# The intermediate words of a float64 conversion move from SBUF to PSUM, and the zero tile gets a place of its own

## The chip, the core and the metric

The kernel runs on one core of a Trainium2 chip. A core has five engines that run side by side and meet through semaphores: TensorE (PE, matmuls into PSUM), VectorE (DVE), ScalarE (ACT), GpSimd (POOL) and SyncE (SP, which here only issues DMAs). SBUF is the large working memory, PSUM the small one of eight banks into which PE writes. The metric is the time of one execution on the device in microseconds (us), the median of several.

## The reference

Three stages follow each other, all in float32 on 2304 tokens (4 batches of 576) of width 512:

```
attention:  8 heads of 64; scores = q k^T / 8 + decay (a difference of prefix sums of log f), causal, softmax, @ v
first MoE:  h = max(x @ w1, x @ w2, x @ w3)  (512 x 768 each);   x = h @ w_out  (768 x 512)
second MoE: gate logits + noise, the best 2 of 8 experts per token;  out += weight * (relu(x @ e1[e]) @ e2[e])
```

The weights of the first MoE (w1, w2, w3, w_out) arrive as float64. They are read as pairs of 32-bit words, and float32 values are made of them on the chip with integer operations.

## The kernel before

The tokens are cut into eight units, two per batch: 256 tokens (scores against 256 keys) and 320 tokens (against 576). Each unit passes through attention, in steps of one tile of up to 128 rows, then the first MoE, then gating; the experts follow when all units are through. All queues are written out by hand: a Python generator issues attention in half steps, and between them the loop over units issues the first MoE's matmuls in 22 groups (18 for the three products, 4 for w_out), so that the attention of the next unit stands between the groups of this one. To keep float32 accuracy most products are made of three matmuls (`three`, L659) on values split into a high and a low part.

The weights of the first MoE are converted in 24 pieces while attention of the first units runs. A piece is a tile `wr` or `raw` of 128 rows with 512 float64 values (two tiles of 256 in two of the late pieces). `w_load` loads it, and `piece` (L325) turns it into float32 with three integer instructions on DVE, with pauses between them:

- L334 shifts the upper words left by 3 and masks them, from the raw tile into the tile `sw`;
- L336 takes sign and top bit of the upper words, ors `sw` into them, and writes them over the upper words in the raw tile;
- L338 shifts the lower words right by 29 and ors the upper words into them, again over the upper words.

Then `split` (L303) writes the high part on ACT (L304) and the low part on POOL (L305). Both words are read with a step of two, since they lie side by side. `sw` is one SBUF buffer of the pool `stg`; the 26 uses (20 tiles `wr` and 2 `raw` of 512 columns, 4 `raw` of 256) share it one after the other. `w_step` issues 0.75 steps of conversion per half step of attention before the first MoE and 1.15 beside it, so the conversions spread over unit 0's and unit 1's attention and end beside unit 0's first MoE.

That MoE sums into tiles `m` (`mtile`, L656) of the PSUM pool `ps_m`, which has three banks used in turn. L680 (ACT) and L682 (DVE) take the maximum of three such sums. Of the attention steps, L457 is DVE's row minimum of the scores, L461 ACT's exponential, L466 and L467 DVE's reciprocal, L469 POOL's scaling, L476 PE's transposes, L488 ACT's copy of them, L530 the product with V in plain float32 for the first 16 heads, and L236 (POOL) and L237 (DVE) the split of q and k for the next head.

`zero_dram` (L149) takes the same buffer as `sw` for a tile `zt` of zeros once the conversions are through, clears `meta` and the first rows of `x2d`, and clears the output in 19 stores of 256 KB, one per three groups of the first MoE from unit 1 on.

Of the kernel before, what the change touches and what calls it, by code (L numbers as in the profile page):

```python
# [8 lines left out]
F32 = mybir.dt.float32  # L9
# [12 lines left out]
DM = 512  # L22
# [11 lines left out]
LN_EXP_SET = [x.name for x in SETS].index("natural_log_exp_and_others")  # L34
XBUF = 8            # attention outputs kept (hi and lo) for the first MoE
STB = 3             # staging buffers
RATE0, RATE1 = 0.75, 1.15   # steps of weight conversion per half step of attention, before and in the first MoE
W0 = 4              # attention step from which weights are converted
WE, PF0, PFD = 1, 4, 3      # weight pieces loaded at once, before conversions start, ahead of them
CN = 1              # attention step at which the decay prefixes are stored  # L40
ND = 4              # heads that get their prefix straight from SBUF
AH = 5              # heads by which the first split heads are loaded ahead
NV = 16             # heads whose P @ V runs in plain float32
LG = 20             # attention step at which the gate's inputs are loaded
VSH = 1             # steps by which V is split later
LEAD = (6, 2)       # attention steps of the next unit done beside a unit's first MoE
GG = 22             # groups of matmuls in a unit's first MoE
PPD, PPL, RSP = 5, 1, 1     # pauses in a unit's gating: before positions (last unit: PPL), between row tiles
HK, TE = (1, 3), (2, 5)     # places of interleaved work in expert 0's products
COLS = ((0, 2 * QA_N), (QA_N, QA_N + S + QB_N))  # L50
# [4 lines left out]
def moe_stack(ctx, tc, qk, v, f, w1, w2, w3, wo, wg, noise, e1, e2, out):  # L55
# [28 lines left out]
    with tc.manual_schedule():  # L84
# [3 lines left out]

        # -------------------------------------------------- attention buffers
        QKA = [ap_.tile([128, QB_N + S], F32R, name=f"QKA{i}") for i in range(2)]  # L90
# [8 lines left out]

        # ------------------------------------------------------ decay prefix  # L100
        BH = B * H
# [10 lines left out]

        # ---------------------------------------------------------- constants
        nc.gpsimd.memset(ident, 1.0)
# [34 lines left out]
        def zero_dram():  # L149
            zt = stg.tile([128, DM], F32, tag="sw", name="zt", bufs=1)  # L150
            nc.gpsimd.memset(zt, 0.0)
            nc.sync.dma_start(meta.rearrange("(p r) t -> p (r t)", p=128), zt[:, 0:NE * REG // 64])
            nc.sync.dma_start(x2d[0:PAD, :], zt)
            for r in range(NTOK // 128 + 1):
                yield
                nc.sync.dma_start(out[r * 128:(r + 1) * 128, :], zt)

        # ---------------------------------------------------------- attention
        XH, XL = {}, {}
# [136 lines left out]
        nc.gpsimd.tensor_scalar(CR[0][:, 1, 0:QA_N], L0.bitcast(F32), -1.0, 0.0, op0=OP.mult, op1=OP.add)  # L296
        # ------------------------------------------------------ MoE1 weights
        moe1_w = {}
# [26 lines left out]
        def piece(raws_, dt, hi_, lo_):  # L325
            n = hi_.free_size() // len(raws_)
            vals = []
            for raw in raws_:
                val = raw[:, 0:n]
                if dt == I64:  # L330
                    r2 = raw.bitcast(I32)[:, 0:2 * n].rearrange("p (c t) -> p c t", t=2)
                    low, top = r2[:, :, 0], r2[:, :, 1]
                    sw = stg.tile([128, 512], I32, tag="sw", name="sw", bufs=1)[:, 0:n]
                    nc.vector.tensor_scalar(sw, top, 3, 0x3FFFFFFF, op0=OP.logical_shift_left, op1=OP.bitwise_and)  # L334
                    yield
                    nc.vector.scalar_tensor_tensor(top, top, -0x40000000, sw, op0=OP.bitwise_and, op1=OP.bitwise_or)  # L336
                    yield
                    nc.vector.scalar_tensor_tensor(top, low, 29, top, op0=OP.logical_shift_right, op1=OP.bitwise_or)  # L338
                    val = raw[:, 0:2 * n].rearrange("p (c t) -> p c t", t=2)[:, :, 1]
                vals.append(val)  # L340
            yield
            for i, val in enumerate(vals):
                split(hi_[:, i * n:(i + 1) * n], lo_[:, i * n:(i + 1) * n], val, nc.gpsimd)
# [310 lines left out]

        # --------------------------------------------------------------- MoE1
        def mtile():  # L656
# [58 lines left out]

        # ------------------------------------------------------------- gating
        scatters = []
# [140 lines left out]

        # ------------------------------------------------------------ experts
        ex = {}  # L860
# [276 lines left out]

        # ------- tokens past the static slots of an expert, or in expert 0's first slots too late for them
        any_ = nc.values_load(anyi[0:1, 0:1], min_val=0, max_val=nxt_t + 1)
# [102 lines left out]
```

## Time and profile before

| | |
|---|---|
| median of 3 runs | 1074.23 us (1074.07 to 1074.79) |
| span of the profiled execution, first to last instruction | 1074.9 us |
| PE busy | 1032.7 us, 96% |
| DVE busy | 550.0 us, 51% |
| ACT busy | 522.2 us, 49% |
| POOL busy | 504.4 us, 47% |
[...]
| first x2T copy of unit 0's first MoE (L711) | 141.1 us |

The page gives no time of the profiled execution besides its span. Busy times are means over the whole span and hide stages; the views by stretch below don't. A matmul's end is modelled, so a busy PE may still contain short stalls. An instruction's duration holds the time in which it stands blocked in the engine, which is why the spread of equal instructions is worth a look.

### The profile page before, as it was taken

Reading aid. Unit: us, or ns where it says so; the run is one execution under the profiler, and the core shown is the slowest. Engines: PE = TensorE matmul, PEld = TensorE weight load, DVE = VectorE, ACT = ScalarE, POOL = GpSimd, SP = SyncE. Lnnn points to the kernel's source line nnn. Section 1 sums busy time; section 2 is a strip of 40 time slices with the busy share of each in tenths; the row PEclk is TensorE's granted clock in tenths of the full one; section 3 lists DMA queues with packets and bytes.
Section 4 is the critical chain, followed back from the end, with each engine's and each line's share of the span. In section 5 each row is a group of like instructions: output and inputs, shape, how many; then the busy total and the mean of one; then the engine's idle time right before and its main releaser. Section 6 shows DMA issues by size and latency. Waiting matters only on the chain.

```text
span 1074.9 us, 18911 instructions
## 1 busy us (share of the span) xinstructions
PE 1032.7 (96%) x6612; PEld 916.6 (85%) x6612; DVE 550.0 (51%) x1505; ACT 522.2 (49%) x1310; POOL 504.4 (47%) x573
## 2 busy tenths in 40 slices
PE   6899899999999999999999999999999999999996
PEld 3466688989989899898899988989898989899995
DVE  6999958658586585865635424323132323223210
ACT  5666656666566675666523334333333333333211
POOL 6778645544645446454327255343434252444202
PEclk9989999999999999999999999999999999999998
DMA  7764434232342212321013247363535354444203
GB/s 192 192 164 133 129 86 136 82 91 86 98 126 61 52 57 59 107 58 46 12 68 121 83 83 213 128 127 108 137 86 141 98 137 118 125 111 119 40 10 41
DMA packets 77167, 109.17 MB, mean 102 GB/s; under 512 B 37172, under 2 KB 38580, under 8 KB 77004
## 3 DMA queue, kind: packets, MB, share of 16 engines
q1 hardware_dynamic: 66828, 86.90, 27.6%
q0 software_dynamic: 10240, 21.02, 10.3%
q8 instruction: 54, 0.88, 0.3%
q14 instruction: 45, 0.37, 0.1%
HBM read 86.48 MB, written 21.39 MB: 100 GB/s over the span
## 4 chain that ended last, share of the span: by engine, by line
PE 74%; DVE 13%; DMA 4%; issue 3%; POOL 3%; ACT 1%; SPq 1%; POOLq 0%; DVEq 0%; ACTq 0%
PE m L660 8%; PE m L662 7%; PE m L661 7%; PE g L660 6%; PE g L661 6%; PE g L662 6%; PE m L973 6%; PE m L972 6%; PE m L971 6%; PE o L534 4%; PE pt L476 3%; DVE wr L336 2%; DVE QKB L237 2%; DMA wr<-in_w 2%; PE m L729 2%
## 5 line engine op out<-in xcount | busy, mean ns | idle before, releaser
L469 POOL TENSOR_SCALAR P<-P,stat 128x512 f32<-128x512 f32 (+4 forms) x160 | 101.4, 634 | 219.3 <-DVE stat L467 125.1
L660 PE MATMUL g<-xTh,eh 128*128 128x384 f32 (+1 forms) x512 | 159.3, 311 | 0.6 <-DVE hl L956 0.6
L661 PE MATMUL g<-xTl,eh 128*128 128x384 f32 (+1 forms) x512 | 158.0, 309 | 0.0
L662 PE MATMUL g<-xTh,el 128*128 128x384 f32 (+1 forms) x512 | 157.9, 308 | 0.0
L978 POOL DMA_INDIRECT out_rows<-ys,dst x40 | 63.1, 1577 | 174.2 <-ACT ys L977 154.2
L305 POOL TENSOR_TENSOR el<-ew,eh 128x1024 fp32r<-128x1024 f32 x36 | 91.6, 2549 | 109.0 <-ACT eh L304 108.9
L956 DVE SCALAR_TENSOR_TENSOR hl<-g,hh 128x384 fp32r<-128x384 f32 (+1 forms) x120 | 58.1, 486 | 130.0 <-ACT hh L955 129.9
L971 PE MATMUL m<-eh,hh 128*128 128x512 f32 x296 | 117.5, 397 | 0.0
L955 ACT ACTIVATE hh<-g 128x384 fp32r<-128x384 f32 (+1 forms) x120 | 52.0, 434 | 131.1 <-PE g L662 126.1
L973 PE MATMUL m<-eh,hl 128*128 128x512 f32 x296 | 115.7, 391 | 0.0
L972 PE MATMUL m<-el,hh 128*128 128x512 f32 x296 | 115.6, 391 | 0.0
L940 DVE TENSOR_TENSOR xTl<-t,xTh 128x512 fp32r<-128x512 f32 x40 | 27.6, 691 | 153.7 <-ACT xTh L939 153.7
L977 ACT ACTIVATE ys<-m,mv 128x512 f32<-128x512 f32 x40 | 27.5, 687 | 157.4 <-issue 124.1
L660 PEld LDWEIGHTS g<-xTh,eh 128*128 128x128 f32 x512 | 96.7, 189 | 1.6 <-DVE hl L956 1.0
L661 PEld LDWEIGHTS g<-xTl,eh 128*128 128x128 f32 x512 | 96.8, 189 | 0.2 <-DVE xTl L940 0.2
L662 PEld LDWEIGHTS g<-xTh,el 128*128 128x128 f32 x512 | 96.7, 189 | 0.0
L502 ACT ACTIVATE PTh<-pt 128x128 fp32r<-128x128 f32 (+2 forms) x120 | 52.3, 436 | 90.0 <-PE pt L476 53.7
L476 PE MATMUL pt<-ident,P 128*128 128x128 f32 x480 | 76.8, 269 | 8.9 <-POOL P L469 6.6
L476 PEld LDWEIGHTS pt<-ident,P 128*128 128x128 f32 x480 | 52.8, 144 | 20.6 <-POOL P L469 12.6
L304 ACT ACTIVATE eh<-ew 128x1024 fp32r<-128x1024 f32 x64 | 67.5, 1056 | 6.0 <-DMA ew<-in_e 6.0
L457 DVE TENSOR_REDUCE stat<-sB 128x1 f32<-128x256 f32 (+2 forms) x80 | 46.2, 577 | 45.2 <-PE sB L451 41.2
L236 POOL TENSOR_TENSOR QKA<-qkraw,QKB 64x576 fp32r<-64x576 f32 (+1 forms) x56 | 67.8, 1210 | 0.0
(316 smaller groups left out, 2954.3 us busy)
## 6 DMA issues: line engine op xcount, KB each, us to landing
ew<-in_e SPq DMA_DIRECT2D x64, 512.0 KB
qkraw<-in_qk SPq DMA_DIRECT2D x64, 224.0 KB
wr<-in_w SPq DMA_DIRECT2D x18, 512.0 KB
qkraw<-in_qk SPq DMA_DIRECT2D x48, 128.0 KB
out_rows<-zt SPq DMA_DIRECT2D x19, 256.0 KB
vr<-in_v SPq DMA_DIRECT2D x37, 128.0 KB
x2d<-row SPq DMA_DIRECT2D x16, 256.0 KB
vr<-in_v SPq DMA_DIRECT2D x24, 64.0 KB
```

The lines of the kernel that those rows point to most:

```text
L236: nc.gpsimd.tensor_tensor(KA[0:64], rk[0:64], KB[0:64].bitcast(F32), op=OP.subtract)
L304: nc.scalar.activation(hi_, raw, AF.Copy)
L305: leng.tensor_tensor(lo_, raw, hi_.bitcast(F32), op=OP.subtract)
L469: nc.gpsimd.tensor_scalar(p, p, st[0:t.w, 3:4], 0.0, op0=OP.mult, op1=OP.add)
L476: nc.tensor.transpose(t.pt[:, j * t.w:(j + 1) * t.w], p[0:t.w, j * 128:(j + 1) * 128], ident[0:t.w, 0:t.w])
L660: nc.tensor.matmul(o, lh, rh, start=first, stop=False)
L661: nc.tensor.matmul(o, lh, rl, start=False, stop=False)
L662: nc.tensor.matmul(o, ll, rh, start=False, stop=last)
L971: nc.tensor.matmul(y, hh, wh[:, f_ % 2, :], start=(f_ == 0), stop=False)
L972: nc.tensor.matmul(y, hh, wl[:, f_ % 2, :], start=False, stop=False)
L973: nc.tensor.matmul(y, hl, wh[:, f_ % 2, :], start=False, stop=(f_ == 7))
L978: nc.gpsimd.indirect_dma_start(out=out[:, :], out_offset=bass.IndirectOffsetOnAxis(ap=ex["dst"][:, e, c:c + 1], axis=0), in_=ys, in_offset ...
```

## The change

Three edits; the rest of the diff takes away comments and blank lines.

- The tile for the intermediate words is taken from `ps_m`, with the tag `m` of the sums of the first MoE, and is called `cv`. It is now one more user of these three banks.
- L336 (L337 of the new numbering) writes its result into that tile and not over the upper words. L338 (L339) reads it there and writes the upper words of the raw tile as before.
- `zt` gets its own place in the pool `const`, with 288 columns instead of 512. The stores that need 512 read 256 of its columns twice.

```
     def zero_dram():
-        zt = stg.tile([128, DM], F32, tag="sw", name="zt", bufs=1)
+        zt = const.tile([128, 1, NE * REG // 64], F32, name="zt")
         nc.gpsimd.memset(zt, 0.0)
-        nc.sync.dma_start(meta.rearrange("(p r) t -> p (r t)", p=128), zt[:, 0:NE * REG // 64])
-        nc.sync.dma_start(x2d[0:PAD, :], zt)
+        nc.sync.dma_start(meta.rearrange("(p r) t -> p (r t)", p=128), zt[:, 0, :])
+        zr = zt[:, :, 0:DM // 2].to_broadcast([128, 2, DM // 2])
+        nc.sync.dma_start(x2d[0:PAD, :].rearrange("p (a c) -> p a c", a=2), zr)
         for r in range(NTOK // 128 + 1):
             yield
-            nc.sync.dma_start(out[r * 128:(r + 1) * 128, :], zt)
+            nc.sync.dma_start(out[r * 128:(r + 1) * 128, :].rearrange("p (a c) -> p a c", a=2), zr)
...
-                    sw = stg.tile([128, 512], I32, tag="sw", name="sw", bufs=1)[:, 0:n]
+                    sw = ps_m.tile([128, 512], I32, tag="m", name="cv")[:, 0:n]
                     nc.vector.tensor_scalar(sw, top, 3, 0x3FFFFFFF, op0=OP.logical_shift_left, op1=OP.bitwise_and)
                     yield
-                    nc.vector.scalar_tensor_tensor(top, top, -0x40000000, sw, op0=OP.bitwise_and, op1=OP.bitwise_or)
+                    nc.vector.scalar_tensor_tensor(sw, top, -0x40000000, sw, op0=OP.bitwise_and, op1=OP.bitwise_or)
                     yield
-                    nc.vector.scalar_tensor_tensor(top, low, 29, top, op0=OP.logical_shift_right, op1=OP.bitwise_or)
+                    nc.vector.scalar_tensor_tensor(top, low, 29, sw, op0=OP.logical_shift_right, op1=OP.bitwise_or)
```

No instruction changes its place on any engine; operands and waits do. On PE, beside unit 0's first MoE, this is the end of one group of sums (w21), the transposes (L476) and scores (L447 to L451) of an attention step, and the first matmuls of the next group (w02). Before:

```order
L662 MATMUL m<-xh,w21l 128x256
L476 MATMUL pt<-ident,P_108 128x64 [waits Activation_49,Pool_49]
L476 MATMUL pt<-ident,P_108 128x64 x4
L447 MATMUL sB<-QKB_94 128x384 [waits Activation_49]
L448 MATMUL sB<-QKA_92 128x384 [waits DMAHW3_49]
L451 LDWEIGHTS identb
L451 MATMUL sB<-trib,identb 128x128
L660 MATMUL m<-xh,w02h 128x256
L661 MATMUL m<-xl,w02h 128x256
```

And now, with lines numbered one higher:

```order
L663 MATMUL m<-xh,w21l 128x256
L477 MATMUL pt<-ident,P_108 128x64 [waits PE_49,Pool_49]
L477 MATMUL pt<-ident,P_108 128x64 x4
L448 MATMUL sB<-QKB_94 128x384 [waits Activation_49]
L449 MATMUL sB<-QKA_92 128x384 [waits DMAHW3_49]
L452 LDWEIGHTS identb
L452 MATMUL sB<-trib,identb 128x128
L661 MATMUL m<-xh,w02h 128x256 [waits DVE_49]
L662 MATMUL m<-xl,w02h 128x256
```

The group's first matmul had no wait of its own: its bank was that of three groups before, and an earlier wait covered its release. It now waits for DVE, which has to empty the sum of the group before last (L682). On DVE, at the place where unit 0's first MoE begins, one conversion between the steps of attention. Before:

```order
L334 TENSOR_SCALAR sw<-wr_102 128x512 [waits DMAHW5_49]
L682 TENSOR_TENSOR t_718<-m,t_718 128x256 [waits Activation_49]
L336 SCALAR_TENSOR_TENSOR wr_102<-wr_102,sw 128x512 [waits DVE_49]
L466 TENSOR_SCALAR stat<-stat 128x1 [waits Activation_49]
L467 RECIPROCAL stat<-stat 128x1 [waits DVE_49]
L457 TENSOR_REDUCE stat<-sB 64x1 [waits PE_49,Pool_49]
L338 SCALAR_TENSOR_TENSOR wr_102<-wr_102 128x512
```

And now:

```order
L335 TENSOR_SCALAR cv<-wr_102 128x512 [waits DMAHW5_49,Activation_49]
L683 TENSOR_TENSOR t_718<-m,t_718 128x256
L337 SCALAR_TENSOR_TENSOR cv<-wr_102,cv 128x512 [waits DVE_49]
L467 TENSOR_SCALAR stat<-stat 128x1 [waits Activation_49]
L468 RECIPROCAL stat<-stat 128x1 [waits DVE_49]
L458 TENSOR_REDUCE stat<-sB 64x1 [waits PE_49,Pool_49]
L339 SCALAR_TENSOR_TENSOR wr_102<-wr_102,cv 128x512
```

The first instruction of the conversion now also waits for ACT, which reads a sum out of the bank (L680); the maximum behind it waited for that same copy before.

## Rows read from the trace of the kernel before

**Rows 1.** The chain that ended last, shares by line, 34 to 140 us.

```profile
by line: DVE sw L334 14.8%; DVE wr L336 14.6%; DVE wr L338 12.4%; DVE stat L457 10.0%; issue 9.9%; DMA wr<-in_w 9.0%; DVE QKB L237 7.4%; PE o L530 3.9%; DVE t L682 3.1%; DVE raw L336 3.0%; DVE hl L690 3.0%; POOL P L469 2.6%; DVE raw L338 1.
```

**Rows 2.** By stretch: busy us of PE, PEld, DVE, ACT, POOL; granted clock, DMA share, GB/s.

```profile
14.00:34.50 20.50, 18.92 (x62) 11.41 (x62) 14.90 (x40) 13.38 (x45) 11.68 (x16) 1.00 1.02 268
34.50:66.00 31.50, 24.20 (x91) 13.44 (x90) 29.10 (x54) 19.31 (x54) 23.12 (x24) 0.84 0.56 150
66.00:140.00 74.00, 67.09 (x452) 51.60 (x451) 71.37 (x137) 48.33 (x128) 55.31 (x50) 1.00 0.47 139
139.00:200.00 61.00, 59.42 (x430) 54.90 (x429) 41.13 (x145) 40.61 (x130) 29.90 (x47) 1.00 0.41 115
```

**Rows 3.** The lines L334, L336, L338: ns min/median/max.

```profile
L334 DVE TENSOR_SCALAR sw<-wr x20: 407/476/2624, 18.2 to 112.2; 128x512 int32<-128x512 int32 x20
...
L336 DVE SCALAR_TENSOR_TENSOR wr<-wr,sw x20: 677/1100/1770, 18.7 to 113.3; 128x512 int32<-128x512 int32 x20
...
L338 DVE SCALAR_TENSOR_TENSOR wr<-wr x20: 674/938/1805, 19.8 to 115.3; 128x512 int32<-128x512 int32 x20
```

**Rows 4.** DVE in order of time, 36 to 42.6 us: start, duration, instruction.

```profile
36.11 0.69 DVE L336 SCALAR_TENSOR_TENSOR wr<-wr,sw 128x512 int32<-128x512 int32 x1
...
39.05 2.62 DVE L334 TENSOR_SCALAR sw<-wr 128x512 int32<-128x512 int32 x1
```

**Rows 5.** POOL in order of time, 38 to 42 us.

```profile
38.02 1.66 POOL L236 TENSOR_TENSOR QKA<-qkraw,QKB 64x576 fp32r<-64x576 f32 x1
39.66 0.47 POOL L469 TENSOR_SCALAR P<-P,stat 128x256 f32<-128x256 f32 x1
40.10 1.28 POOL L305 TENSOR_TENSOR w20l<-wr,w20h 128x512 fp32r<-128x512 f32 x1
```

**Rows 6.** DVE by line and shape, 18 to 140 us: busy, mean ns | idle before.

```profile
L682 DVE TENSOR_TENSOR t<-m,t 128x256 f32<-128x256 f32 x12 | 4.9, 410 | 0.0
...
L690 DVE TENSOR_TENSOR hl<-t,hh 128x256 fp32r<-128x256 f32 x6 | 4.0, 668 | 0.5 <-ACT hh L686 0.5
```

**Rows 7.** DVE by line and shape, 140 to 600 us.

```profile
L509 DVE TENSOR_TENSOR PTl<-pt,PTh 128x512 fp32r<-128x512 f32 x24 | 16.4, 683 | 4.1 <-ACT PTh L502 4.0
```

**Rows 8.** DVE's busy time on tile wr (L334, L336, L338) by stretch.

```profile
14.00:34.50 20.50, 10.32 (x12) 1.00 1.02 268
34.50:66.00 31.50, 17.40 (x17) 0.84 0.56 150
66.00:140.00 74.00, 31.60 (x31) 1.00 0.47 139
```

**Rows 9.** The same on tile raw.

```profile
66.00:140.00 74.00, 13.44 (x18) 1.00 0.47 139
```

**Rows 10.** PE in order of time, the ten matmuls of two heads.

```profile
60.43 4.30 PE L530 MATMUL o<-PTf,vr 128*64 128x320 f32 x10
...
70.68 2.41 PE L530 MATMUL o<-PTf,vr 128*64 128x320 f32 x10
```

**Rows 11.** PE in order of time: first matmuls of three groups.

```profile
73.02 0.38 PE L660 MATMUL m<-xh,w20h 128*128 128x256 f32 x1
...
109.56 0.36 PE L660 MATMUL m<-xh,w02h 128*128 128x256 f32 x1
...
135.87 0.39 PE L660 MATMUL m<-hh,wo0h 128*128 128x256 f32 x1
```

**Rows 12.** DVE in order of time: what these groups would wait for.

```profile
71.45 1.78 DVE L338 SCALAR_TENSOR_TENSOR wr<-wr 128x512 int32<-128x512 int32 x1
...
111.89 0.41 DVE L682 TENSOR_TENSOR t<-m,t 128x256 f32<-128x256 f32 x1
...
135.79 0.50 DVE L338 SCALAR_TENSOR_TENSOR raw<-raw 128x256 int32<-128x256 int32 x1
```

**Rows 13.** The zero tile: ns min/median/max, first and last start.

```profile
L156 SPq DMA_DIRECT2D out_rows<-zt x19: 337/383/577, 155.6 to 311.3; - x19
L151 POOL MEMSET zt<- x1: 529/529/529, 148.5 to 148.5; 128x512 f32 x1
```

## The prediction

> **What bounds the kernel now.** I read the profile from the whole to the place of the change. Over the span TensorE (PE) is busy nearly all the time, so a kernel of this sort is normally moved only by what moves PE. The slices of the page show one exception: early on, VectorE (DVE) is as full as PE. So I took the chain that ended last over just that stretch, 34 to 140 us: the reader is to see that the three conversion lines L334, L336 and L338 hold about 45% of it, more than all matmuls together [rows 1]. The busy times by stretch say why [rows 2]. From 14 to 34.5 us the DMA engines are full (share 1.02). From 34.5 to 66 us DVE is busy 29.1 of 31.5 us, from 66 to 140 us 71.4 of 74 us, PE 24.2 and 67.1. From 139 us, when the last weight is converted, PE has 59.4 of 61 us and DVE falls to 41.1. Hence the conversion sets the pace from 34.5 to about 139 us and nothing does so after it but PE.
>
> Next question: are those instructions long by their work or by waiting? The same shape of L336 takes from 677 to 1770 ns, of L334 from 407 to 2624 ns [rows 3]. The timeline shows what fills the difference. With GpSimd (POOL) silent, L336 at 36.11 takes 0.69 us. L334 at 39.05 takes 2.62 us; three POOL instructions stand back to back from 38.02 to 40.10 + 1.28 = 41.38 us, and L334 ends 0.29 us behind the last of them [rows 4, 5]. So it did no visible work until POOL was silent, and then took less than its fastest case. L336 and L338 with two SBUF sources do the same. The counterexample is on the same engine and in the same 122 us: L682, whose sources are one PSUM and one SBUF tile, has a mean of 410 ns for 128x256, while L690 of the same size with two SBUF sources has 668 [rows 6]. A source in PSUM is what tells the undisturbed from the disturbed ones.
>
> **The change, part by part.** The order of instructions is the same on all engines; three things differ.
>
> *Place of the words.* All 78 conversion instructions (66 of 512 columns, 12 of 256) now have at most one SBUF source and one PSUM tile. L334 goes SBUF to PSUM, L336 SBUF and PSUM to PSUM, L338 SBUF and PSUM to SBUF. No row of before writes PSUM from DVE. The nearest rows read it: L509 with one PSUM and one SBUF source, 128x512, mean 683 ns, and L682 128x256, 410 ns [rows 6, 7]. I take 683 and 410 for all three. The ends: as fast as the best now (407 ns for L334, 677 for L336 [rows 3]), or as slow as the stretched means now, 1.0 us, if writing PSUM leaves the blocking in place.
> The sum by stretch, busy now from [rows 8, 9]:
> 14 to 34.5 us: 10.32 us in 12 instructions, then 12 x 0.683 = 8.2; 2.1 less, worth nothing, since the loads set the pace there.
> 34.5 to 66 us: 17.40 us in 17, then 17 x 0.683 = 11.6; 5.8 less.
> 66 to 140 us: 31.60 in 31 and 13.44 in 18, of which 12 narrow; then 37 x 0.683 + 12 x 0.410 = 30.2; 14.8 less.
>
> [...]
>
> [...]
>
> What is late next. In 34.5 to 66 us DVE would hold 23.3 of 31.5, PE 24.2 at a granted clock of 0.84, POOL 23.1 and shorter itself, as it no longer waits behind the conversions. The chain there runs from one DVE instruction to the next, so the 5.8 us come off nearly whole: 6 with what POOL gives. [...]
> In 66 to 140 us DVE would fall to 56.6 and PE is next: 6.9 us idle now. From 139 to 200 us PE still idles 1.6 of 61, which is about 1.8 in such a stretch. So 5.1 of the 14.8 can be had; matmul ends are modelled, so PE may hide some stall in its busy time, and I keep 9 as the far end. I take 5.
>
> *The three banks.* The tile cv takes its turn in the pool ps_m, whose three banks held only the sums of the first MoE. Before 66 us nobody else uses them. Beside unit 0's first MoE, the first matmul of a group must now find an earlier conversion finished, or the sum of the group before last evacuated. Laid on the times of before, ten of its groups would start before that release: the first by 0.21 us (73.02 against 71.45 + 1.78), the most by 2.74 (109.56 against 111.89 + 0.41), the last by 0.42 (135.87 against 135.79 + 0.50); all ten sum to 10.5 us [rows 11, 12]. Queued behind such a matmul on PE are transposes and scores of the next attention step, and for the scores waits DVE's L457. But each of these releases is itself a DVE instruction behind the conversions, or ScalarE's copy L680, and DVE's are earlier by the sum above, up to 20 us at the end, where PE would ask 11 us earlier. A group and its share of attention take 3.9 us (73.02 to 135.87 us for 16 groups), DVE's part of that, now 71.4 of 74, would be 56.6 of 74, 3.0 us; so PE finds its bank free but for the odd case. I charge nothing beyond the 1.8 us of idle left above; the other end is all 10.5. DVE's own new waits (a bank whose sum ScalarE or DVE reads) had ended before it got there in every case, in the times of before.
>
> *The zero tile.* POOL's memset shrinks from 512 to 288 columns (529 ns now), and 20 stores send two runs of 1 KB per row instead of one of 2 KB. The nineteen into out_rows are issued from 155.6 to 311.3 us, where DMA has room (0.41 from 139 to 200 us [rows 2]) and nothing but the far later scatter-adds needs them; SP issues one in 383 ns at the median [rows 13]. Nothing gained or lost; if the finer runs doubled the issue, 19 x 0.38 = 7 us of SP, spread over 160 us, would lie in a queue that waits anyway. Comments and blank lines move line numbers only.
>
> Sum: 6 + 5 = 11 us off the profiled span of 1074.9, that is 1063.9. The median of the runs lies 0.7 below that span, so 1063.
>
> **Rivals.**
> The banks eat the second stage: PE waits about as long as it is spared, and only the 6 us of the first stay: 1068. For it: ten late releases. Against it: the releasers move forward with the change.
> The banks make it slower: PE and DVE take turns, each group waiting for a conversion and each score for the group. Price 10.5 us in the second stage, against the 6 in the first: 1079. It decides where a conversion instruction still takes about 1 us, so that DVE keeps its present lag behind PE. Against it are L509 and L682, undisturbed all along.
> The change doesn't do what it says: POOL still blocks, for instance because the one SBUF source is enough. Then L334 loses its fast form, 22 x 0.27 = 6 us of DVE at most, part of it given back where PE is next, and the time is 1073 to 1078, likeliest 1074. Against it: L682's 410 beside L690's 668.
> [...]
>
> **How the numbers follow.** Forecast 1063 with its own range 1058 to 1067: 0.62. Second stage eaten, 1068: 0.18. More, 1057: 0.08. No effect, 1074: 0.07 (0.05 of it inside 0.2%). Slower, 1079: 0.05. From 1056 to 1071 holds the first three but for the edges, some 0.86 and a little less for sizes I haven't thought of. A measurement of this kernel can tell 0.2%, 2.1 us, from nothing. Faster: 0.62 + 0.18 + 0.08 = 0.88. Same: 0.05. Slower: 0.05 + 0.02 = 0.07.
>
> **What would show it.** Right: L335, L337 and L339 of the new numbering at 0.68 us with hardly any spread, beside POOL at work; DVE near 85% of 34 to 130 us, (23.3 + 56.6) / 94.5; the first x2T copy some 11 us earlier, and the stages behind it as long as before. Wrong: the conversions spread up to 2 us still (the blocking is not about the second SBUF source), or PE's wait for a conversion among its longest in 60 to 130 us (the banks), or the gain there by 140 us and gone at the end.

## The result, and the profile after

The changed kernel takes 1064.0 us, median of four runs (1063.6 to 1064.7), against 1074.3 for the kernel before on the same chip: a ratio of 0.9905, 95% interval 0.9891 to 0.9919. 1063 was predicted. The profiled execution has a span of 1062.1 us against 1074.9.

First the conversion lines, in the view of one line's instructions (ns min/median/max, first and last start), in the changed kernel:

```profile
L335 DVE TENSOR_SCALAR cv<-wr x20: 675/684/699, 18.1 to 102.5; 128x512 int32<-128x512 int32 x20
...
L335 DVE TENSOR_SCALAR cv<-raw x6: 420/428/695, 106.2 to 124.0; 128x256 int32<-128x256 int32 x4, 128x512 int32<-128x512 int32 x2
...
L337 DVE SCALAR_TENSOR_TENSOR cv<-wr,cv x20: 678/695/697, 18.9 to 103.8; 128x512 int32<-128x512 int32 x20
...
L339 DVE SCALAR_TENSOR_TENSOR wr<-wr,cv x20: 671/679/692, 19.9 to 105.4; 128x512 int32<-128x512 int32 x20
```

Where equal instructions once took from 407 to 2624 ns [rows 3], the widest of the three lines on tile `wr` now spans 24 ns. (The line on `raw` mixes two shapes.) That POOL is still at work beside them shows in the timeline of the changed kernel, DVE first:

```profile
37.77 0.70 DVE L335 TENSOR_SCALAR cv<-wr 128x512 int32<-128x512 int32 x1
...
38.50 0.69 DVE L337 SCALAR_TENSOR_TENSOR cv<-wr,cv 128x512 int32<-128x512 int32 x1
...
40.55 1.11 DVE L238 SCALAR_TENSOR_TENSOR QKB<-qkraw,QKB 64x320 fp32r<-64x320 f32 x1
```

and POOL in the same stretch:

```profile
38.16 1.30 POOL L306 TENSOR_TENSOR w20l<-wr,w20h 128x512 fp32r<-128x512 f32 x1
...
39.89 1.42 POOL L237 TENSOR_TENSOR QKA<-qkraw,QKB 64x576 fp32r<-64x576 f32 x1
```

L337 runs whole within POOL's L306 (38.16 to 39.46 us) and takes 0.69 us. L238, which keeps two SBUF sources, starts within POOL's L237 and ends 0.35 us behind it, at 41.66: the old picture [rows 4, 5], on an instruction that the change left alone. DVE's busy time on tile wr by stretch was 10.32, 17.40 and 31.60 us in 12, 17 and 31 instructions [rows 8]; now it is

```profile
14.00:34.50 20.50, 9.47 (x14) 1.00 1.01 272
34.50:66.00 31.50, 13.12 (x20) 0.84 0.73 191
66.00:140.00 74.00, 18.36 (x27) 1.00 0.48 135
```

The busy times by stretch that answer to [rows 2] (PE, PEld, DVE, ACT, POOL; granted clock, DMA share, GB/s):

```profile
14.00:34.50 20.50, 18.88 (x67) 11.65 (x67) 14.14 (x42) 13.90 (x49) 10.43 (x16) 1.00 1.01 272
34.50:66.00 31.50, 25.11 (x124) 15.69 (x125) 28.32 (x64) 23.19 (x63) 23.02 (x27) 0.84 0.73 191
66.00:140.00 74.00, 72.03 (x510) 58.44 (x509) 59.06 (x149) 51.44 (x143) 47.25 (x59) 1.00 0.48 135
139.00:200.00 61.00, 59.98 (x420) 54.48 (x418) 42.49 (x148) 39.81 (x121) 29.55 (x46) 1.00 0.40 111
```

A caution for readers: stages move with a change, and a fixed window then holds something else. In the 74 us from 66 the changed kernel spends its last 10 us in the next stage. The stage itself, from the first matmul of the first MoE to the first x2T copy (ACT's copy that brings unit 0's result out of PSUM), before:

```profile
65.67:141.05 75.38, 68.47 (x463) 52.93 (x463) 72.05 (x140) 49.55 (x132) 56.47 (x51) 1.00 0.47 138
```

and after:

```profile
60.20:129.39 69.19, 67.22 (x463) 52.78 (x463) 59.03 (x140) 49.65 (x132) 46.18 (x51) 1.00 0.54 153
```

The same 463 matmuls and 140 DVE instructions: DVE sheds 13.0 us, of which the stage gives back 6.2, and PE fills 97% of it. PE's busy time and its idle time add up to the stage: busy fell from 68.5 to 67.2 us, idle from 6.9 to 2.0. The chain that ended last, 34 to 140 us, by line, against [rows 1]:

```profile
by line: PE o L531 12.6%; PE m L661 7.7%; PE m L663 6.8%; PE m L662 6.4%; DMA raw<-in_wo 6.0%; issue 5.8%; PE pt L477 5.3%; DVE cv L337 4.9%; DMA qkraw<-in_qk 4.7%; DVE stat L458 4.6%; DVE wr L339 4.4%; DVE cv L335 4.3%; DMA vr<-in_v 4.0%; 
```

The three conversion lines fall from about 45% to about 14%, and loads (qkraw, vr, wo) come in. The banks hardly matter here. What PE waited for from 60 to 130 us (total, times, longest):

```profile
PE m L661 <- DVE stat L467: 0.9, 2, 0.6
PE sA L449 <- DMA QKA<-cum: 0.7, 1, 0.7
PE m L663 <- POOL wo2l L306: 0.3, 1, 0.3
```

The 0.9 us are two waits for a bank. L467 only ended last; one bank was released by a maximum (L683, 0.3 us), the other by a conversion (L339, 0.6 us), each some 0.06 us before the matmul began.

Followed through the kernel, the lead over before is 5.5 us where the first MoE starts, 11.7 at the first x2T copy, 13.3 at the seventh unit's, 15.3 at the eighth's, and 12.8 at the end. So the gain comes where it was forecast; what happens behind 200 us was not, and is taken up below.

### The profile page after: what moved, and what is told of

It reads as the page before. It is cut to its first block, busy times and chain, and to the rows that moved or that the text cites. A ratio compares the mean times of both kernels' runs of the same rounds, so it can differ in the third digit from the quotient of the medians.

```text
span 1062.1 us, 18914 instructions
## 1 busy us (share of the span) xinstructions
PE 1028.4 (97%) x6612; PEld 912.7 (86%) x6612; DVE 528.8 (50%) x1505; ACT 521.9 (49%) x1310; POOL 488.9 (46%) x573
## 4 chain that ended last, share of the span: by engine, by line
PE 80%; DVE 8%; DMA 4%; issue 3%; POOL 2%; ACT 1%; SPq 1%; POOLq 0%; DVEq 0%; ACTq 0%
PE m L661 9%; PE m L663 8%; PE m L662 8%; PE g L661 6%; PE g L662 6%; PE g L663 6%; PE m L974 6%; PE m L973 6%; PE m L972 6%; PE pt L477 4%; PE o L535 4%; PE o L531 2%; PE m L730 2%; PE t L938 2%; PE sB L448 1%
## 5 line engine op out<-in xcount | busy, mean ns | idle before, releaser
L470 POOL TENSOR_SCALAR P<-P,stat 128x512 f32<-128x512 f32 (+4 forms) x160 | 92.7, 579 | 214.9 <-DVE stat L468 103.7
L306 POOL TENSOR_TENSOR el<-ew,eh 128x1024 fp32r<-128x1024 f32 x36 | 91.9, 2556 | 106.8 <-ACT eh L305 106.7
L458 DVE TENSOR_REDUCE stat<-sB 128x1 f32<-128x256 f32 (+2 forms) x80 | 46.2, 577 | 47.2 <-PE sB L452 39.0
L974 PEld LDWEIGHTS m<-eh,hl 128*128 128x128 f32 x296 | 55.6, 188 | 13.2
L973 PEld LDWEIGHTS m<-el,hh 128*128 128x128 f32 x296 | 55.7, 188 | 11.9
```

Source lines behind the costliest of these rows:

```text
L306: leng.tensor_tensor(lo_, raw, hi_.bitcast(F32), op=OP.subtract)
L470: nc.gpsimd.tensor_scalar(p, p, st[0:t.w, 3:4], 0.0, op0=OP.mult, op1=OP.add)
L973: nc.tensor.matmul(y, hh, wl[:, f_ % 2, :], start=False, stop=False)
L974: nc.tensor.matmul(y, hl, wh[:, f_ % 2, :], start=False, stop=(f_ == 7))
```

## The experiments

Theory at the start (T): DVE and POOL shut each other out while a DVE instruction lives on SBUF alone, an operand in PSUM frees it, and what DVE sheds is gained until PE is the bound. All ratios are to the kernel before on the same chip. What the profiles showed, in one table ("starts" is the first matmul of the first MoE; the stage runs from there to the first x2T copy; "PE idle" is the stage less PE's busy time; times in us):

| kernel | ratio (95%) | starts | stage | DVE busy in it | PE busy in it | PE idle in it |
|---|---|---|---|---|---|---|
| before | 1 | 65.67 | 75.38 | 72.05 | 68.47 | 6.91 |
| changed | 0.9905 (0.9891 to 0.9919) | 60.20 | 69.19 | 59.03 | 67.22 | 1.97 |
| e1 store form | 1.0009 (0.9999 to 1.0019) | 65.23 | 75.29 | 71.85 | 68.49 | 6.80 |
| e2 words only | 0.9881 (0.9862 to 0.9900) | 60.95 | 68.75 | 59.33 | 67.50 | 1.25 |
| e3 third step | 0.9912 (0.9895 to 0.9928) | 57.80 | 70.93 | 63.24 | 67.86 | 3.07 |
| e4 first step | 0.9944 (0.9928 to 0.9961) | 63.56 | 72.55 | 65.43 | 69.03 | 3.52 |
| e5 first twice | 1.0002 (0.9993 to 1.0012) | 61.25 | 75.82 | 70.94 | 69.37 | 6.45 |
| e7 slower rate | 0.9934 (0.9922 to 0.9946) | 57.54 | 74.05 | 65.93 | 68.56 | 5.49 |
| e8 zero tile 256 | 0.9881 (0.9864 to 0.9898) | 59.80 | 69.27 | 59.32 | 67.49 | 1.78 |
| e9 sums in PSUM | 1.0166 (1.0150 to 1.0181) | 60.02 | 75.56 | 59.20 | 67.38 | 8.18 |
| e10 faster rate | 0.9978 (0.9967 to 0.9990) | 70.05 | 67.33 | 53.59 | 66.29 | 1.04 |
| e12 wo earlier | 0.9888 (0.9868 to 0.9908) | 55.78 | 68.58 | 59.62 | 67.45 | 1.13 |
| e13 changed again | 0.9902 (0.9889 to 0.9916) | 56.77 | 68.86 | 59.20 | 67.19 | 1.67 |
| e14 last unit | 0.9887 (0.9872 to 0.9902) | 58.65 | 68.96 | 59.74 | 67.51 | 1.45 |

### The parts of the change: e1 and e2

e1 is the kernel before with the stores of the zero tile as in the changed one:

```
-            zt = stg.tile([128, DM], F32, tag="sw", name="zt", bufs=1)
+            zt = stg.tile([128, 1, NE * REG // 64], F32, tag="sw", name="zt", bufs=1)
...
-                nc.sync.dma_start(out[r * 128:(r + 1) * 128, :], zt)
+                nc.sync.dma_start(out[r * 128:(r + 1) * 128, :].rearrange("p (a c) -> p a c", a=2), zr)
```

e2 is the changed kernel with the zero tile and its stores as before:

```
-            zt = const.tile([128, 1, NE * REG // 64], F32, name="zt")
+            zt = stg.tile([128, DM], F32, tag="sw", name="zt", bufs=1)
...
-                nc.sync.dma_start(out[r * 128:(r + 1) * 128, :].rearrange("p (a c) -> p a c", a=2), zr)
+                nc.sync.dma_start(out[r * 128:(r + 1) * 128, :], zt)
```

> The kernel before with only the zero tile's new form: 288 columns instead of 512, each store of 2 KB rows sent as two runs of 1 KB; the conversion as before. My theory (T): VectorE and GpSimd shut each other out while a VectorE instruction reads and writes SBUF alone, and the gain comes from giving each of the three conversion steps an operand in PSUM; the stores have no part in it. T expects 1074, between 1073 and 1075, all stages as long as before. Rival Z (the stores carry a part, either way: a shorter memset and earlier issue gain, or 1 KB runs cost in the experts' stages): outside that, and then in the stages behind 155 us, where the stores are issued.

> The changed kernel with the zero tile as it was before (512 columns, 2 KB rows, in the staging pool): the words alone. T expects 1064, between 1063 and 1065, and L335, L337, L339 at 0.68 us without spread. Rival Z: between 1066 and 1073, since a part of the 10 us would be the zero tile's; or, if the 1 KB runs cost, below 1062. The stages of the experts, 0.57 us longer each in the changed kernel's profile than in the one of before, tell whether the stores did that: by Z they are as short as before here.

e1: 1075.44 us beside 1075.17, no difference that can be told. SP issues a store in 592 ns at the median instead of 383 [rows 13], 4 us of SP in all, and no stage is more than 0.3 us longer. e2: 1062.81 us, a ratio of 0.9881. The words carry the whole gain, and perhaps more: the interval lies below that of the changed kernel but for a small overlap, which T did not foresee.

### Which operand matters: e3 and e4

e3 is the changed kernel with two SBUF sources in the third step again:

```
-                    nc.vector.scalar_tensor_tensor(sw, top, -0x40000000, sw, op0=OP.bitwise_and, op1=OP.bitwise_or)
+                    nc.vector.scalar_tensor_tensor(top, top, -0x40000000, sw, op0=OP.bitwise_and, op1=OP.bitwise_or)
...
-                    nc.vector.scalar_tensor_tensor(top, low, 29, sw, op0=OP.logical_shift_right, op1=OP.bitwise_or)
+                    nc.vector.scalar_tensor_tensor(top, low, 29, top, op0=OP.logical_shift_right, op1=OP.bitwise_or)
```

e4 has the first word in SBUF and the second in PSUM (`cv`), on e2:

```
+                    s1 = stg.tile([128, 512], I32, tag="sw", name="sw", bufs=1)[:, 0:n]
...
-                    nc.vector.tensor_scalar(sw, top, 3, 0x3FFFFFFF, op0=OP.logical_shift_left, op1=OP.bitwise_and)
+                    nc.vector.tensor_scalar(s1, top, 3, 0x3FFFFFFF, op0=OP.logical_shift_left, op1=OP.bitwise_and)
...
-                    nc.vector.scalar_tensor_tensor(sw, top, -0x40000000, sw, op0=OP.bitwise_and, op1=OP.bitwise_or)
+                    nc.vector.scalar_tensor_tensor(cv, top, -0x40000000, s1, op0=OP.bitwise_and, op1=OP.bitwise_or)
```

> The changed kernel, but the second step (L337) writes its word over the weights in SBUF as before, so that the third (L339) has two SBUF sources again, while the first two keep a PSUM operand. T: L339 alone is stretched again (mean about 0.94 us, up to 1.8, as L338 before), the other two stay at 0.68; of the 22.9 us that the three lines lost to blocking in the kernel before, 7.3 are L338's, so about a third of the gain goes: 1067, between 1065.5 and 1069. Rival B (it is writing to PSUM, not the sources' place, that frees the engines, so an instruction that writes SBUF is blocked): L337 is stretched too, 1068 to 1071. [...]

> The other way round: the first step writes SBUF (one SBUF source, SBUF result, as before), the second has two SBUF sources and writes PSUM, the third has one SBUF and one PSUM source. Zero tile as before. T: the first step is 0.41 to 2.6 us again, the second 0.68 to 1.1 and more although it writes PSUM, the third 0.68 without spread: about two thirds of the gain go, 1071, between 1069 and 1073. Rival B (the result's place decides): the second step is at 0.68 without spread, and the time is 1067 to 1069. Rival N (only the first step's form counts): all of the gain goes, 1073 to 1075.

The three lines of e3, ns min/median/max:

```profile
L335 DVE TENSOR_SCALAR cv<-wr x20: 673/682/696, 17.8 to 101.8; 128x512 int32<-128x512 int32 x20
...
L337 DVE SCALAR_TENSOR_TENSOR wr<-wr,cv x20: 669/687/696, 18.5 to 103.2; 128x512 int32<-128x512 int32 x20
...
L339 DVE SCALAR_TENSOR_TENSOR wr<-wr x20: 681/902/1602, 19.6 to 105.2; 128x512 int32<-128x512 int32 x20
```

and of e4:

```profile
L335 DVE TENSOR_SCALAR sw<-wr x20: 407/526/2977, 18.1 to 107.2; 128x512 int32<-128x512 int32 x20
...
L337 DVE SCALAR_TENSOR_TENSOR cv<-wr,sw x20: 679/976/1805, 18.6 to 108.2; 128x512 int32<-128x512 int32 x20
...
L339 DVE SCALAR_TENSOR_TENSOR wr<-wr,cv x20: 669/679/692, 19.7 to 110.2; 128x512 int32<-128x512 int32 x20
```

Exactly the instructions that T named are stretched. L337 decides between the theories: in e3 it writes SBUF and has one SBUF source, and is undisturbed (669 to 696 ns); in e4 it writes PSUM and has two SBUF sources, and is stretched to 1.8 us (679 to 1805 ns). So for this instruction the sources decide, not the result's place (rival B falls), and not the first step's form alone (rival N falls). The first step is another case: L335 has one SBUF source in both kernels, and is undisturbed where it writes PSUM (e3, 673 to 696 ns) and stretched where it writes SBUF (e4, 407 ns at best, 2977 at most). The times came out some 2 us lower than expected, e3 just below its range: a us of stretch costs less than a us, as the next group shows.

### What a us of DVE is worth: e5, e7 and e10

e5 issues the first step a second time, right behind the first:

```
                     nc.vector.tensor_scalar(sw, top, 3, 0x3FFFFFFF, op0=OP.logical_shift_left, op1=OP.bitwise_and)
+                    nc.vector.tensor_scalar(sw, top, 3, 0x3FFFFFFF, op0=OP.logical_shift_left, op1=OP.bitwise_and)
```

e7 converts later:

```
-RATE0, RATE1 = 0.75, 1.15
+RATE0, RATE1 = 0.55, 1.3
```

and e10, on e8 (the zero tile of 256 columns, below), earlier:

```
-RATE0, RATE1 = 0.75, 1.15
+RATE0, RATE1 = 1.0, 1.15
```

> The changed kernel with the first conversion step (L335) issued twice: 20 more instructions of 0.686 us and 6 of 0.42 to 0.69, that is 16.8 us more of VectorE, nothing else. T says that after the change VectorE still sets the pace of the first stage (28.3 of 31.5 us busy from 34.5 to 66 us) but no longer that of the second, where TensorE has 72.0 of 74 us and VectorE 59.1. Some 9 of the added instructions fall before the first MoE starts; those beside the full DMA queues cost nothing. T: 3 to 5 us in the first stage, 0 to 3 in the second: 1069, between 1067 and 1072. Rival (VectorE is still the bound in both stages, so the gain was simply VectorE's time): 15 to 17 us, 1079 to 1081. Rival (TensorE bounds both): no change, 1064 to 1065.

> The changed kernel with other rates of conversion: RATE0 0.55 for 0.75 before the first MoE, RATE1 1.3 for 1.15 beside it. T: conversions move from the stretch where VectorE is the bound to the one where it has 15 us left. About a quarter of the some 18 conversion instructions between 34.5 and 60 us, 3 to 4 us of VectorE, leave the first stage, and cost nothing in the second as long as TensorE finds its weights in time: 1061, between 1059.5 and 1063. Rival W (weights come too late: TensorE waits for a converted weight in the second stage, as the code demands all six of a quarter before its first group): 1064 to 1067, with a wait of TensorE for L339 or L306 among its longest.

> The kernel with the 256-column zero tile, and RATE0 at 1.0 for 0.75: more of the conversion before the first MoE, the opposite of the other rate experiment. Revised theory (R), after the doubled step and the slower rate both missed: the first stage, from 14 us to the first MoE, is no longer VectorE's after the change (6.9 us more of it cost 0.75 us there), it waits for loads (vr 4.26 us, qkraw 5.03 us in the chain) and for TensorE at half clock; the second stage still pays for VectorE's time, 6.6 us for 10.1 in the doubled step, 4.9 us for 5.5 in the slower rate, 6.2 us for 15.1 in the change itself. So conversion belongs in the first stage: some 8 instructions, 5.5 us, leave the second, which becomes 2 to 5 us shorter, and cost 0.5 to 1.5 us in the first: 1060, between 1058 and 1062. Rival (the first stage is paid for too: in the chain of the changed kernel VectorE stands without a gap from 35 to 45 us): the gain and the price cancel, 1062 to 1064. Rival (the converted weights' loads crowd out the attention's loads): the first stage is longer by 3 us or more, 1064 to 1067.

All three missed: e5 takes 1075.09 us, e7 1068.55 and e10 1072.45. e5 took back the whole gain. Of the 9.9 us between its profile and that of the changed kernel, 6.6 lie in the stage beside the MoE, where T expected 0 to 3. Another 1.8 lie in the last unit (from the seventh unit's first x2T copy to the eighth's), but there e13, the changed kernel run once more, takes the same 46.23 us as e5. The MoE starts 1.05 us later; seven profiles of kernels alike up to there start it anywhere from 55.78 to 60.95 us (see e13), so one profile can't tell what the doubled step costs ahead of it. T had read the slack from the fixed window of 66 to 140 us, which is the mistake named above. In its stage, 75.82 us long, e5 has DVE at 94% and PE at 91%, neither full:

```profile
61.25:137.07 75.82, 69.37 (x463) 54.19 (x463) 70.94 (x157) 49.82 (x132) 45.71 (x51) 0.98 0.50 139
```

Two lines of PE's waits in this stage are for the banks of the pool `ps_m`, 3.7 us together:

```profile
PE m L662 <- DVE stat L468: 3.2, 2, 2.4
...
PE m L662 <- DVE wr L340: 0.5, 1, 0.5
```

In all three cases L340, the last step of a conversion, ended some 0.05 us before the matmul began; L468 only ended later by the profile. So with the doubled step the banks come free later, too, and e5 doesn't show the price of DVE's time alone. POOL is as little busy in e5's stage as in the changed kernel's (45.7 and 46.2 us), so its relief alone doesn't carry the gain; what share it has was not tried.

The table puts the price of DVE's time in this stage together. From 53.6 us (e10) to 59.0 (changed) the stage grows by 1.9, from there to 63.2 (e3) by 1.7, and from 63.2 to 72.05 (before) by 4.5: about 0.34, 0.41 and 0.51 us for each us of DVE. That the price falls is not shown: six profiles of the changed stage (changed, e2, e8, e12, e13, e14) lie between 68.58 and 69.27 us, which is as much as sets these figures apart. PE holds the floor, with 66.3 (e10) to 67.2 us (changed) busy; DVE's work is paid for in part above it, since attention goes from PE to DVE and back in each step. e4 lies 0.5 us above this line, e5 1.0 and e7 1.8 (65.93 and 74.05); in all three the granted clock of the stage is 0.98, in the four others 1.00. In e7 PE waited for

```profile
PE m L661 <- DVE stat L467: 2.1, 2, 1.3
PE m L661 <- DVE raw L339: 1.8, 1, 1.8
PE m L661 <- DVE wr L339: 1.1, 2, 0.6
```

That looks like rival W, PE waiting for a converted weight, but it is not. The longest of these waits, in order of time on DVE, PE and ACT:

```profile
126.38 0.42 DVE L339 SCALAR_TENSOR_TENSOR raw<-raw,cv 128x256 int32<-128x256 int32 x1
...
126.86 0.38 PE L661 MATMUL m<-hh,wo0h 128*128 128x256 f32 x1 [1.79 <-DVE raw L339]
...
127.82 0.41 ACT L305 ACTIVATE wo2h<-raw 128x256 fp32r<-128x256 f32 x1
```

The matmul reads wo0, split by 112.84 us, and starts 0.06 us behind the last step of a conversion of wo2, which ACT splits only a us later. What it waited for is the bank that `cv` held. The other four are the same: w10, w21, w02 and w22 had been split 6.8 us or more before. These waits are 5.0 of PE's 5.5 us of idle time in e7, and 0.9 of 2.0 in the changed kernel. So the conversions, crowded together beside the MoE, brought the price that the prediction's rivals on the banks had feared.

e10 shortened the stage by 1.9 us against e8, just under what theory R said, but its MoE starts 10.25 us later, and its time lies above all the ranges given. Both rivals have a part in that. DVE's waits for weights from 14 us to that start in e10:

```profile
DVE cv L336 <- DMA wr<-in_w: 8.4, 4, 4.3
```

and from 14 to 60 us in e8:

```profile
DVE cv L336 <- DMA wr<-in_w: 3.7, 3, 1.7
```

Behind these waits DVE is full:

```profile
40.00:70.00 30.00, 23.55 (x82) 13.43 (x82) 29.11 (x56) 18.94 (x51) 21.08 (x24) 0.83 0.59 151
```

The ten conversion instructions more are 6.9 us, the longer waits for weights 4.7. e5 has ten more there too, 6.9 us, but no earlier loads; DVE waits 1.5 us for weights and the MoE starts at 61.25 us, not 70.05. So neither shift paid: earlier, conversion waits for loads and fills DVE; later, it holds PE's banks.

### Where the zero tile lies: e8 and e13

e8 cuts the zero tile from 288 columns to 256, and the store to `meta` reads 144 of them twice; e13 is the changed kernel once more.

```
-            zt = const.tile([128, 1, NE * REG // 64], F32, name="zt")
+            zt = const.tile([128, 1, DM // 2], F32, name="zt")
```

> The changed kernel with the zero tile at 256 columns instead of 288 (the stores read it twice over), which moves every tile allotted after it by 128 bytes per partition: 1024 bytes of zeros instead of 1152. In the changed kernel's profile, and in that of the third-step experiment, which has the same layout, the second matrix products of the experts (L972 to L974) follow each other at 231 to 237 ns instead of 227 in the kernel before and in the words-alone experiment, and each expert is 0.57 us longer. Theory A (the place of the tiles in SBUF does that, and it goes by 256 bytes: the tiles behind the staging pool moved by 896 bytes, which is no multiple): here they move by 1024, the pitch is 227 again, each expert is as long as before, and about 4 us go: 1060 to 1062. Rival (the new stores or chance do it): pitch 231 to 237 and 1064.

> The changed kernel unaltered, beside the next one on the same chip. In the profiles so far the first stage ended between 55.8 and 61 us with the same program up to there, with 6.8 to 24 us of it at half clock. If the difference between this kernel (0.9905 of before) and the words alone or the 256-column zero tile (0.9881 each) is the place of the tiles, it stays: 1064, between 1063 and 1065, 0.989 to 0.992 of before, and the second products of the experts at 231 to 237 ns. If it was chance of the first stage, the runs spread from 1060 to 1065 as theirs do, 0.988.

PE's second products of the experts in the changed kernel, in order of time:

```profile
700.74 0.40 PE L974 MATMUL m<-eh,hl 128*128 128x512 f32 x1
...
701.44 0.39 PE L974 MATMUL m<-eh,hl 128*128 128x512 f32 x1
```

and in e8:

```profile
700.59 0.39 PE L975 MATMUL m<-eh,hl 128*128 128x512 f32 x1
...
701.26 0.39 PE L975 MATMUL m<-eh,hl 128*128 128x512 f32 x1
```

Three matmuls take 0.70 us with the 288-column tile and 0.67 to 0.68 with the 256-column one. The median distance from one to the next is 231 to 233 ns for the three lines in all the kernels with the tile of 288 columns (changed, e3, e5, e7, e9, e13), and 227 ns in all the others (before, e1, e2, e4, e8, e10, e12, e14). The 237 of the expectations is no median: single distances in the changed kernel gather near 230 and near 237. Each expert is 0.57 us longer with it, 4 us over seven. On the other hand e8 and e2 lose 0.26 us per unit against it from the first x2T copy to the seventh unit's, 1.6 in all, so some 2.4 us remain. That fits the difference between 0.9881 (e2, e8) and 0.9905 or 0.9902 (the changed kernel, twice), but the runs don't settle it: the intervals overlap, and e8's median is 1063.9 us (1060.42 to 1064.41), where its rival had it and not theory A, 0.9896 of the median of the kernel before. The shorter distance is shown, a shorter total time is not. The place of the tiles in SBUF is what these kernels differ in, not the stores, since e1 and e8 have the short stores and 227 ns. The shifts tried are two, 1152 bytes with the longer distance and 1024 with the shorter; that it goes by 256 bytes was the author's guess, and these two runs fit it without showing it. Which of the operands feels it was not tried.

e13 also shows what chance does ahead of the MoE. The same program starts it at 56.77 us instead of 60.20. In the changed kernel's first profile the granted clock was 0.53 over these ten matmuls ahead of it (54.88 to 59.26 us):

```profile
54.88 4.38 PE L531 MATMUL o<-PTf,vr 128*64 128x320 f32 x10
...
60.20 0.36 PE L661 MATMUL m<-xh,w00h 128*128 128x256 f32 x1
```

and in e13, with a granted clock of 1.00 from 34.5 to 66 us against 0.84:

```profile
53.44 2.39 PE L531 MATMUL o<-PTf,vr 128*64 128x320 f32 x10
...
56.77 0.36 PE L661 MATMUL m<-xh,w00h 128*128 128x256 f32 x1
```

Seven profiles with the same order of instructions up to there (changed, e2, e8, e9, e12, e13, e14) start the MoE between 55.78 and 60.95 us. The clock is part of it (1.99 us in these ten matmuls), but e12 has the earliest start with a clock of 0.87; what else differs stays open.

### Attempts at a faster kernel: e9, e12 and e14

e9 keeps the last maximum in its bank, where `hi_part` and `lo_part` read it; e14 does that on e12 for the last unit alone (u == 7):

```
-                            nc.vector.tensor_tensor(t1[:, 0:n], ph[:, 0:n], t1[:, 0:n], op=OP.max)
+                            nc.vector.tensor_tensor((ph if i == 2 else t1)[:, 0:n], ph[:, 0:n], t1[:, 0:n], op=OP.max)
...
-                    def lo_part(f_=f_, t1=t1):
+                    def lo_part(f_=f_, t1=ph):
```

e12, on e8, loads the first four of the six pieces of wo one conversion earlier:

```
-            while nload[0] < len(wsrc) and nload[0] <= n + (PFD if nload[0] < 18 else 2):
+            while nload[0] < len(wsrc) and nload[0] <= n + (PFD if nload[0] < 18 else 3 if nload[0] < 22 else 2):
```

> The changed kernel with the same idea in one more place: the last maximum of a group of the MoE (L683, i = 2) is written back into its PSUM bank, so that the subtraction L691, which had two SBUF sources, reads PSUM and SBUF. T: in the changed kernel L691 took 5.79 us once at 559.8 us, beside GpSimd's weights, against 0.41 to 0.49 otherwise; in the words-alone experiment such a stretch (2.71 us at 571.0) kept TensorE waiting for 1.9 us. L691 stays at 0.42 and 0.49 us everywhere; 0 to 2 us less: 1063, between 1062 and 1065. Rival (the bank is held until the subtraction, two group steps longer, and TensorE waits for one of the three banks): 1065 to 1075, with waits of L661 for L691 among TensorE's longest.

> The kernel with the 256-column zero tile, and the loads of the output weights wo issued one conversion earlier (three ahead for two). In the changed kernel's chain two waits for these loads stand, 2.90 us at 108.19 and 3.47 us at 117.92, behind SyncE's loads L204 and L206, which wait in the same queue for TensorE to release V; one conversion earlier they stand ahead of those. If the loads end the second stage (theory L): it is 2 to 6 us shorter, 1059, between 1057 and 1061. If they only come at the same time as the work of VectorE and TensorE that ends it anyhow (theory R): 0 to 1.5 us, 1061 to 1063. Rival (the wo loads now wait in the queue for their buffer ahead of the heads' loads, which come late): 1063 to 1066.

> The kernel with the 256-column zero tile and the wo loads one conversion earlier, and the sum kept in PSUM (L683, L691 reading PSUM) in the last unit alone, where no attention stands beside the MoE. There L691 with two SBUF sources took 5.7 us and then 2.9 to 3.4 us beside GpSimd in the profiles of both predecessors, and the stage from the seventh unit's first x2T copy to the eighth's took 46.43 us; in the changed kernel's own profile, where the second stretch didn't happen, 44.46. T: L691 at 0.49 us there, the stage 44.4 to 45.7, so 0.8 to 2 us less: 1061, between 1058 and 1063, 0.986 to 0.988 of before. Rival (the banks held two group steps longer cost TensorE as much as in the kernel that kept the sums in PSUM everywhere): the stage 46.4 or longer, and no gain, 1062 to 1064.

e9 takes 1093.42 us, 1.7% more than the kernel before and some 29 us more than the changed one, worse than its rival said. L691 does lose its stretch (483 to 492 ns in the last unit), but PE then waits for banks in every unit. Its waits from 60 to 602 us:

```profile
PE m L661 <- ACT t L681: 15.3, 11, 1.9
PE m L661 <- ACT row L760: 4.9, 5, 1.0
PE m L661 <- DVE hl L691: 4.2, 4, 1.6
```

e12 brought 0.7 us in the stage, no more than profiles of the same stage differ by, and nothing that the runs can tell: theory R. In e14 the stretch in the last unit went, from e13's

```profile
555.90 5.78 DVE L691 TENSOR_TENSOR hl<-t,hh 128x320 fp32r<-128x320 f32 x1 [0.54 <-issue]
564.89 2.83 DVE L691 TENSOR_TENSOR hl<-t,hh 128x320 fp32r<-128x320 f32 x1 [2.07 <-ACT hh L687]
```

to a maximum of 493 ns, but PE waited once for the bank instead:

```profile
PE m L662 <- DVE hl L692: 1.6, 1, 1.6
```

and the stage takes 46.40 us, as without it: the rival. Beside e13 on the same chip it has 1062.8 us against 1064.0, with overlapping runs and intervals. None of the kernels tried is clearly ahead of the changed one; e2 and e8, both at 0.9881, come nearest, 0.2% below it, with the reserve made above for e8.

## Why the prediction was right

**Durations.** 683 and 410 ns were taken; 684, 695, 679 and 411 to 429 were measured. DVE's conversion takes 49.9 us in all, 40.95 on wr and 8.93 on raw, where the three stretches of the sum make 50.0. L334's 407 ns, its best with source and result in SBUF, became 684 with the result in PSUM, and L336's 677, its best with two SBUF sources, became 695.

**The first stage**, forecast 6: 5.5 between two profiles with the same granted clock in the fixed window, 0.84, and 8.9 in e13, at 1.00. The mechanism was right and its end was not: where the conversions shrank, loads came into the chain. From 34 us to the MoE's start in the changed kernel:

```profile
by line: DMA qkraw<-in_qk 19.2%; DMA vr<-in_v 16.3%; PE o L531 16.0%; DVE QKB L238 9.4%; DVE stat L458 7.5%; DVE wr L339 7.5%; DVE cv L337 5.3%; issue 4.8%; DVE cv L335 4.7%; ACT P L462 3.5%; PE sB L448 2.8%; PE pt L477 2.2%; ACT w01h L305 
```

DVE is busy 28.3 of 31.5 us, not 23.3, since later work moved into the window. The clock, which the sum leaves out, was 0.84 and 1.00 in this window in two profiles of the same program, and the ten matmuls of L531 took 4.38 and 2.39 us in them, so that 5.5 came so near to 6 is in part luck.

**The second stage**, forecast 5: 6.2, and 6.5 in e13. PE next was right, at 97%. The sum was PE's idle time less what would remain, 6.9 - 1.8 = 5.1; measured were 6.9 - 2.0 = 4.9. The other 1.3 us are PE's busy time, 68.5 to 67.2, the hidden stalls that the prediction left for its far end of 9. The cap was not the end either: with 5.7 us of DVE less than e8, e10's stage is another 1.9 shorter.

**The banks**, charged nothing: right, 0.9 us of waits for a bank, within the 1.8 left idle. Their releases came forward with the conversions. The margin is narrow: 3.7 us with one step doubled (e5), 5.0 with the conversions closer together (e7), and e9 shows the price when something holds a bank for two group steps.

**The zero tile**, charged nothing: this is the step that was wrong. The stores cost nothing (e1). But the tile's new place moved the tiles behind it, and the second products of the experts follow each other some 2% more slowly (231 to 233 ns against 227). It stayed small because the units gained a part of it back.

**Tests.** The three lines are at 0.68 to 0.70 us beside POOL, as said. DVE is busy 83.45 of the 96 us from 34 to 130, 87%, forecast 85. The first x2T copy is 11.7 us earlier, forecast 11. The stages behind are not as long as before: the last unit was 2.0 us shorter in this profile, by chance (46.23 us in e13, 46.46 before), and the experts 4 us longer. One sign of being wrong came up by its words: a wait for a conversion is among PE's longest from 60 to 130 us. But it is one wait of 0.6 us.

**Sum.** 11 us forecast off the profiled span, 12.8 measured there; 10.3 between the medians. Two errors meet here: the gain by the first x2T copy is larger than said, 11.7 us and 15.4 in e13, and the tile's place takes back some 2 us. That they nearly cancel is luck; the mechanism, DVE freed from POOL and PE next, is not.

## What to carry to other kernels

Where equal DVE instructions differ by a factor of two or more in their durations, look at POOL beside them and count their SBUF sources. Moving one of two sources to PSUM cured it here (L336 from up to 1770 ns to 697 at most, L338 from 1805 to 692), and so did moving the result of the one-source step (L334, from up to 2624 ns to 699), as long as the bank was free soon. Read a stage by its own first and last instruction, not by a fixed window, before saying which engine is next, and expect the saved time of one engine to be worth a part of itself: 13.0 us of DVE brought 6.2. Before a wait is called one for data, look when the data were ready: in e7 they had long been, and the wait was for a bank. When a tile changes its size or pool, compare the untouched stages too: the tiles behind it have moved, and here each expert took 0.57 us longer.

## What the runs showed of the hardware

- The conversion's instructions of 128x512 on DVE took about as long where they write PSUM (684 and 695 ns, medians of L335 and L337) as where L339 writes SBUF with a PSUM source (679).
- POOL gains as well when DVE stops shutting it out: its scaling of 128x512 (L469, now L470) takes 694 ns in the mean up to 130 us, against 1007 up to 140 us before. Of DVE's instructions that keep two SBUF sources, the one on 64x320 (L237, now L238) got longer, 1325 ns against 916, and the one on 128x256 (L690, now L691) shorter, 504 against 668.
- Matmuls of 128x512 in the experts follow each other at 227 ns or at 231 to 233 (medians), and the difference found between the eight kernels and the six is where their tiles lie in SBUF.
